# A residual quantizer on one core: constants on other engines, an overlap copied instead of loaded, and a third add by DMA

## The chip, the cores and the metric

The kernel runs on one core of a Trainium2 chip. The metric is the device time of one execution in microseconds.

## The reference

The input `x` has 2 sequences of 16000 positions with 512 channels, in bf16. The reference computes

- `z = silu(x[t-1]*w0 + x[t]*w1 + x[t+1]*w2)`, a depthwise convolution with three taps for each channel;
- four stages of residual quantization: for each position the nearest of 8 code words of the stage (by `|r|^2 - 2 r.c + |c|^2`, the first one on a tie) is taken from the residual `r`, which starts as `z`; the sum of the four chosen words is `q`;
- `y`, the same kind of three-tap convolution over `q` with the decoder's taps.

All roundings to bf16 on the way count, since a choice of word depends on them.

## The kernel before

The 32000 positions are laid out as 128 rows of 250 groups: row `p` holds positions `250 p` to `250 p + 249`, and group `g` is the 128 positions `250 p + g`. The 250 groups are worked in 17 chunks (`SIZES`: 4, 12, fourteen of 16, and 10). Channels lie on the partitions in four blocks of 128 (`i` = 0 to 3).

For each chunk:

- **Loading.** The buffer `XT` (two of them) holds the chunk's groups and one neighbour on each side, transposed. Chunks 0 and 1 come as rows (`RES` is borrowed for them), are transposed by TensorE (L366) and copied by VectorE and ScalarE (L371, L373). From chunk 2 on, SP's queue issues one DMA transpose per group, G + 2 for a chunk of G (L395).
- **Front.** Per block: three products `Z`, `T`, `T` (VectorE, L449), two additions into `Z` (either a DMA that adds, issued by POOL, or VectorE: L455, L457), the exponential, `+1` and reciprocal on ScalarE (L461, L466, L162; the `+1` of block 3 on VectorE, L468), and the product with `Z` into `RES` (VectorE, L476). From chunk 2 on, the first addition of every block goes by DMA, and the second one in blocks 0 and 1 (`DMA_ADDS`, `DMA_MORE`).
- **Four stages.** TensorE multiplies the residual with itself and with the code words (L540, L545); VectorE takes the norms (L553) and ScalarE the products (L556) out of PSUM; six small steps of VectorE find the first nearest word (L574 to L601); the one-hot is turned (L611, L618) and made into pairs (L626, L631); TensorE picks the words, in three bf16 parts `W` for each pair of words (L653); VectorE updates the residual (L659).
- **Output.** TensorE multiplies the one-hots with the decoder's words (L676), ScalarE copies them out of PSUM into `YSB` (two buffers, L682), and SP's queue stores them (L686).

Constants are made at the start: the mask and the presets of `KEY` and `OH`, the code columns in `RES` (`code_columns`, L227 and L228), the spreads, the word pairs (`pair_rows`, `pair_words`, L278 to L293) and the decoder's words (`taps_of`, `on_words`).

The order of the instructions on each engine is written down by a planner (`Plan.run`) while the kernel is built. Each task has an engine, a time that it holds it, a delay to its result, needs, a due time and buffers that it takes and gives. The planner plays the tasks forward in time and lets each engine take, of those that are ready, the one with the earliest due time. Planner engines such as `ACC`, `OUT`, `ROWS` and `WORDS` are only names: a DMA add is issued by POOL but planned on `ACC`, a store is issued by SP but planned on `OUT`. The order is then fixed: at run time each engine works through its list and waits where something isn't there. Due times come from `PERIOD` (of a chunk), `LEAD`, `SPREAD` (between blocks), `AFTER` (reciprocals), `STAGE` (between stages) and `LATE` (output).

Of the kernel before, what the change touches and what calls it, by code (L numbers as in the profile page):

```python
# [11 lines left out]
F32 = mybir.dt.float32  # L12
ALU = mybir.AluOpType
ACT = mybir.ActivationFunctionType
# [4 lines left out]
GC = 16  # L19
# [4 lines left out]

SIZES = [4, 12] + [16] * 14 + [10]

# [96 lines left out]
def kernel(  # L123
# [46 lines left out]
    for n, G in enumerate(SIZES):  # L170
# [7 lines left out]
    CB4 = const.tile([P, D], BF16, name="CB4")  # L178
    nc.sync.dma_start(out=CB4, in_=bass.AP(tensor=codebooks.tensor, offset=codebooks.offset,
                                             ap=[[0, J], [D, NC], [1, D]]))  # L180
# [44 lines left out]

    def code_columns(t):
        nc.vector.tensor_copy(t[:, :, :, 0:LC], CBT[:, :, :, 0:LC].to_broadcast([P, KT, 2 * GC, LC]))  # L227
        nc.vector.tensor_copy(t[:, :, :, LC + HT:], CBT[:, :, :, LC:].to_broadcast([P, KT, 2 * GC, LC]))  # L228

# [23 lines left out]
    def mask():  # L253
        for h in range(2):
            for r in range(GB):
                nc.vector.tensor_scalar(out=MASK[h * HT:(h + 1) * HT, r, :], in0=IDENT[h * HT:(h + 1) * HT, h * HT:(h + 1) * HT],
                                        scalar1=-1.0, scalar2=-FAR, op0=ALU.add, op1=ALU.mult)
# [22 lines left out]

    def pair_words(s):
        t = ypool.tile([P, J, D], out.dtype, name="YSB").rearrange("p j d -> p (j d)")
        full, left = t[:, 0:2 * D].bitcast(F32), t[:, 2 * D:4 * D].bitcast(F32)
        ends = t[:, 0:2 * D].rearrange("p (d e) -> p d e", e=2)
# [3 lines left out]
        nc.vector.tensor_scalar(out=ends[:, :, 0], in0=low, scalar1=-1.0, scalar2=None, op0=ALU.mult)  # L288
        nc.vector.tensor_tensor(out=ends[:, :, 1], in0=third, in1=high, op=ALU.subtract)
        nc.vector.tensor_copy(low, full)  # L290
        nc.vector.tensor_tensor(out=left, in0=full, in1=low, op=ALU.subtract)
        nc.vector.tensor_copy(high, left)
        nc.vector.tensor_tensor(out=third, in0=left, in1=high, op=ALU.subtract)  # L293

# [6 lines left out]
    def presets(n):  # L301
        for c in range(C):
            nc.vector.memset(KEYS[n][1][:, :, c, 0], float(C - c))
        nc.vector.memset(OHB[n], 0.0)

# [10 lines left out]
    def taps_of(name):  # L316
        t, first, tap, count = PARTS[name]
        nc.vector.memset(t, 0.0)
        src = bass.AP(tensor=dw_dec.tensor, offset=dw_dec.offset + tap * D, ap=[[D, count], [0, NC], [1, D]])
        nc.gpsimd.dma_start(out=t[first * NC:(first + count) * NC, :], in_=src)  # L320
# [5 lines left out]
    early = -4.0 * PERIOD  # L326
    words_in = plan.add("WORDS", 3.5, 3.5, [], early, lambda: None)
    codes = [plan.add("DVE", 0.3, 0.5, [words_in], early, code_words)]
    codes[0] = plan.add("DVE", 1.2, 1.4, codes, early + 2.0, lambda: code_columns(RESB[0]))
    scored = [plan.add("DVE", 2.4, 2.6, [], early + 1.0, mask), plan.add("DVE", 1.9, 2.1, [words_in], early + 1.0, code_norms)]  # L330
    preset = [plan.add("DVE", 0.8, 1.0, [], early + 2.0 if n == 0 else 0.1 * PERIOD, lambda n=n: presets(n)) for n in range(3)]
    spread = plan.add("DVE", 1.5, 1.7, [], 0.2 * PERIOD, spreads)
    words = []
    for n in range(Nq - 1):
        t = plan.add("DVE", 0.2, 6.0, [], (0.05 + 0.3 * n) * PERIOD, lambda n=n: pair_rows(n))
        words.append(plan.add("DVE", 5.0, 5.2, [t], (0.3 + 0.35 * n) * PERIOD, lambda n=n: pair_words(n), take=("Y",), give=("Y",)))
    codes.append(plan.add("DVE", 1.2, 1.4, [codes[0]], 0.1 * PERIOD, lambda: code_columns(RESB[1])))
    decoder = []
    for n, name in enumerate(PARTS):
        t = plan.add("DVE", 0.2, 6.0, [], (0.3 + 0.02 * n) * PERIOD, lambda name=name: taps_of(name))  # L340
        decoder.append(plan.add("DVE", 0.35, 0.45, [t], 0.5 * PERIOD, lambda name=name: on_words(name)))
    DEC = {name: v[0] for name, v in PARTS.items()}
# [12 lines left out]
    def load_rows(st, org):  # L355
# [29 lines left out]
    def load(st, org):  # L385
        g0, G, GP = st["g0"], st["G"], st["GP"]
        done = []
        if st["n"] < 2:
            load_rows(st, org)
            return  # L390

        def one(n):
            if n == 0:
                st["XT"] = xpool.tile([P, KT, GC + 2, P], BF16, name="XT")
            nc.sync.dma_start_transpose(out=st["XT"][:, :, n, :], in_=group_rows(g0 + n - 1))  # L395

        def edge(n):
            st["XE"] = const.tile([P, KT, P], BF16, name="XE")
            nc.sync.dma_start_transpose(out=st["XE"], in_=group_rows(0))

        def shift(n):
            XT, XE = st["XT"], st["XE"]
            nc.gpsimd.tensor_copy(XT[:, :, n, 0:P - 1], XE[:, :, 1:P])
            for b in range(B):
                p = (b + 1) * HB - 1
                nc.gpsimd.memset(XT[:, :, n, p:p + 1], 0.0)
            if GP > G:
                nc.gpsimd.memset(XT[:, :, G + 2:GP + 2, :], 0.0)

        for n in range(G + 2):  # L410
            due = org - 2.2 * PERIOD + 0.01 * n
            inside = 0 <= g0 + n - 1 < S
            t = plan.add("SP", 1.4, 2.2, done[-1:], due, (lambda n=n: one(n)) if inside else (lambda n=n: edge(n)),
                         take=("XT",) if n == 0 else ())
            done.append(t)
            if not inside:
                st["edge"] = plan.add("POOL", 1.0, 1.4, [t], due, lambda n=n: shift(n))
        st["loaded"] = [done[-1], st.get("edge")]

    def front(st, org):  # L420
# [20 lines left out]
        def block(i):  # L441
# [78 lines left out]
    def stage(st, s, due):  # L520
# [39 lines left out]
        for n in range(banks):  # L560
            m = -(-(G - q) // (banks - n))
            needs = [st["new"][i] for i in range(KT)]
            needs += scored[0:2] + ([codes[st["n"]]] if st["n"] < 3 else [])
            t = plan.add("PE", 0.05 + 0.25 * m, 0.25 + 0.25 * m, needs, due, lambda q=q, m=m: score(q, m), take=("psG",),
                         give=("RES",) if s == Nq - 1 and q + m == G else (), use=0.7)
# [211 lines left out]
```

## Time and profile before

| | |
|---|---|
| median of 3 runs | 797.56 us (787.12 to 799.63) |
| profiled execution | 797.84 us, span 796.1 us, mean granted clock 0.900 |
| busy: VectorE, ScalarE, TensorE | 672.9, 575.3, 565.2 us |
| DMA adds by POOL, transposes, stores of 512 KB | 90, 264, 61 |

In the lines, PE is TensorE, PEld its weight loads, DVE VectorE, ACT ScalarE, POOL GpSimd and SP the engine whose queue issues most of the DMAs. A group's row has its line, engine, operation, tiles and count, then busy time and the mean ns of one, then the idle time just before and what ended it. A row of waits has the total, the count and the longest.

### The profile page before, as it was taken

The page shows a single profiled execution, that of the slowest core. Times are in us where ns is not written, and L with a number is a line of the kernel's source. Part 1 is how long each engine was busy: PE and PEld are TensorE (multiplying, and loading weights), DVE is VectorE, ACT ScalarE, POOL GpSimd, SP SyncE. Part 2 cuts the span into 40 slices and gives each one's busy share as a digit, 9 for nine tenths or more (in the row PEclk, how much of TensorE's full clock was granted, in tenths as well). Part 3 has the DMA queues.
Part 4 walks back from the last instruction along what each step waited for, and adds up shares of the span by engine and source line. Part 5 has one row for each costly group of instructions (what it writes and reads, how often), then busy time and mean ns, then how long its engine had stood idle before and what let it go on. Part 6 is the DMA issues. An engine that isn't in the chain of part 4 may idle for free. (4 is left out here: it accounts for less than half of the span.)

```text
span 796.1 us, 24168 instructions
## 1 busy us (share of the span) xinstructions
PE 565.2 (71%) x10688; PEld 323.2 (41%) x10751; DVE 672.9 (85%) x1249; ACT 575.3 (72%) x658; POOL 98.4 (12%) x116
## 2 busy tenths in 40 slices
PE   3036776667667677777786877777774887888885
PEld 3012443244433444343444444444532444454542
DVE  4899688988978998698978999999995999999851
ACT  1519763869489795779779597989684898777454
POOL 1301002010201101010110111011110121100000
PEclk9557799769899999899988999989997899999999
DMA  7614869795999998899996799899989864422133
GB/s 194 113 26 76 164 100 177 143 155 127 169 159 203 201 168 144 175 172 187 138 229 137 132 203 174 172 203 190 193 144 195 145 166 115 114 75 81 55 135 133
DMA packets 167571, 119.08 MB, mean 150 GB/s; under 512 B 146921, under 2 KB 147306, under 8 KB 167338
## 3 DMA queue, kind: packets, MB, share of 16 engines
q1 hardware_dynamic: 153252, 69.77, 42.9%
q0 software_dynamic: 14064, 47.63, 34.6%
q8 instruction: 84, 1.38, 0.7%
q14 instruction: 21, 0.17, 0.1%
q10 hardware_dynamic: 150, 0.13, 0.1%
HBM read 3.70 MB, written 32.77 MB: 46 GB/s over the span
## 5 line engine op out<-in xcount | busy, mean ns | idle before, releaser
L659 DVE TENSOR_TENSOR RES<-RES,SEL 128x2048 bf16<-128x2048 bf16 (+2 forms) x204 | 222.5, 1137 | 29.9 <-PE SEL L653 29.4
L545 PEld LDWEIGHTS <-RES 128*64 128x64 bf16 x8064 | 164.2, 117 | 113.6 <-issue 84.0
L545 PE MATMUL PS<-RES 128*64 128x80 bf16 (+1 forms) x8064 | 189.8, 207 | 21.1 <-DVE RES L476 11.3
L653 PE MATMUL SEL<-OHP,W 64*128 64x512 bf16 (+2 forms) x1224 | 159.3, 393 | 33.6 <-ACT OHP L631 12.6
L455 POOL DMA_DIRECT2D Z<-T x90 | 86.3, 973 | 579.2 <-ACT PR L556 83.4
L682 ACT ACTIVATE YSB<-Y 128x1024 bf16<-128x1024 f32 (+1 forms) x126 | 125.7, 1025 | 31.2 <-DMA out_dram<-YSB 14.6
L461 ACT ACTIVATE E<-Z 128x2048 bf16<-128x2048 bf16 (+2 forms) x68 | 121.5, 1789 | 27.1 <-DVE Z L457 26.0
L553 DVE TENSOR_REDUCE TR<-PS 128x6 bf16<-128x384 f32 (+2 forms) x188 | 95.3, 510 | 30.3 <-PE PS L545 16.9
L162 ACT ACTIVATE E<-E 128x2048 bf16<-128x2048 bf16 (+2 forms) x68 | 119.4, 1787 | 0.2
L556 ACT ACTIVATE PR<-PS 128x48 bf16<-128x48 f32 (+2 forms) x188 | 37.2, 209 | 106.5 <-PE PS L545 68.5
L653 PEld LDWEIGHTS <-W 64*128 64x128 bf16 x1224 | 61.6, 100 | 108.8 <-issue 71.0
L449 DVE TENSOR_SCALAR T<-XT,WENC 128x2048 bf16<-128x2048 bf16 (+2 forms) x136 | 96.5, 717 | 9.5 <-DMA Z<-T 8.7
L676 PE MATMUL Y<-A,OHT 128*128 128x512 bf16 x225 | 79.7, 393 | 20.0 <-ACT YSB L682 7.4
L540 PE MATMUL PS<-MASK,IDENT 128*128 128x384 bf16 (+2 forms) x188 | 61.6, 328 | 44.6 <-ACT PR L556 23.5
L466 ACT ACTIVATE E<-E 128x2048 bf16<-128x2048 bf16 (+2 forms) x51 | 90.9, 1787 | 0.2
L476 DVE TENSOR_TENSOR RES<-Z,E 128x2048 bf16<-128x2048 bf16 (+2 forms) x68 | 77.4, 1140 | 3.4 <-ACT E L162 3.2
L676 PEld LDWEIGHTS <-OHT 128*128 128x128 bf16 x373 | 33.1, 99 | 66.7 <-issue 31.3
L457 DVE TENSOR_TENSOR Z<-Z,T 128x2048 bf16<-128x2048 bf16 (+2 forms) x46 | 46.8, 1018 | 7.7 <-DMA Z<-T 7.7
L611 PE MATMUL ps_oh<-IDENT,OH 128*128 128x128 bf16 x252 | 27.2, 231 | 36.7 <-DVE OH L601 31.0
L449 DVE TENSOR_SCALAR Z<-XT,WENC 128x2048 bf16<-128x2048 bf16 (+2 forms) x68 | 48.4, 714 | 5.6 <-issue 5.3
L350 PE MATMUL PS<-CB,IDENT 128*128 128x512 bf16 x130 | 45.5, 444 | 7.8 <-ACT PR L556 6.3
L618 ACT ACTIVATE OHT<-ps_oh 128x512 bf16<-128x512 bf16 (+2 forms) x68 | 38.2, 566 | 16.1 <-PE ps_oh L611 15.6
(87 smaller groups left out, 389.7 us busy)
## 6 DMA issues: line engine op xcount, KB each, us to landing
Z<-T POOLq DMA_DIRECT2D x84, 512.0 KB, 6.5
out_dram<-YSB SPq DMA_DIRECT2D x61, 512.0 KB, 4.1
XT<-in_x_dram SPq DMA_TRANSPOSE x263, 4.4
Z<-T POOLq DMA_DIRECT2D x6, 384.0 KB, 5.1
RES<-in_x_dram SPq DMA_DIRECT2D x1, 1536.0 KB, 11.2
RES<-in_x_dram SPq DMA_DIRECT2D x1, 640.0 KB, 6.4
W<-in_codebooks_dram POOLq DMA_DIRECT2D x6, 64.0 KB, 5.5
W<-in_codebooks_dram POOLq DMA_DIRECT2D x3, 128.0 KB, 5.2
```

The source lines that it names most:

```text
L162: nc.scalar.add_instruction(mybir.InstActivation(name=nc.get_next_instruction_name(), engine=mybir.EngineType.Activation, ins=args, outs=[ ...
L449: nc.vector.tensor_scalar(out=places(u[name]), in0=taps(i, k), scalar1=WENC[:, i, k:k + 1], scalar2=None, op0=ALU.mult)
L455: nc.gpsimd.dma_start(out=z, in_=t, accum_op=ALU.add)
L461: nc.scalar.activation(u["E"][:, 0:G, :], u["Z"][:, 0:G, :], ACT.Exp, scale=-1.0)
L466: nc.scalar.activation(e, e, ACT.Copy, bias=1.0)
L476: nc.vector.tensor_tensor(out=st["RES"][:, i, 0:2 * G, LC:LC + HT], in0=halves(u["Z"]), in1=halves(u["E"]), op=ALU.mult)
L545: nc.tensor.matmul(V[h * HT:(h + 1) * HT, r, :], lhsT=half[:, LC:LC + HT], rhs=half[:, lo:hi], start=False, stop=(i == KT - 1), skip_group ...
L553: nc.vector.tensor_reduce(out=u["TR"][:, q:q + m], in_=u["V", q][:, :, own:own + HT], axis=AX.X, op=ALU.max)
L653: nc.tensor.matmul(SEL[:, r, 0:R * HT], lhsT=WORDS[s][k][rows, i * P:(i + 1) * P], rhs=u["OHP"][rows, 0:R * HT], start=(k == 0), stop=(k = ...
L659: nc.vector.tensor_tensor(out=now, in0=now, in1=sel[:, :, 0:G, :], op=ALU.add)
L676: nc.tensor.matmul(Y[:, h, :], lhsT=lhs(), rhs=rhs, start=(a == 0), stop=(a == len(terms) - 1))
L682: nc.scalar.activation(u["YSB"][:, k:k + n, :], u[k][:, 0:n, :], ACT.Copy)
```

## The change

- **Constants.** The mask, the presets and the zeroing of the decoder's words go from VectorE to POOL. Of the eight steps for each word pair, three go from VectorE to ScalarE (`even_end` and the two `part`; `guard`, `odd_end` and `remainder` stay on VectorE), and the steps are planned one by one, the first pair at the start. The spreads and the code columns are due at the start.
- **Start.** The codebook is loaded from ScalarE's queue, the two small row pieces from SP's queue, ahead of the large ones.
- **Third chunk's transposes.** Chunk 2 takes its `XT` only after chunk 1's rows have theirs.
- **Two groups copied.** From chunk 2 on, the first two groups of `XT` are copied by ScalarE from the last two of the chunk before (L431, `overlap`), so that a chunk of G groups needs G transposes: 234 instead of 264.
- **One more add by DMA.** `DMA_MORE` is 3: the second addition of block 2 goes by DMA too, 105 instead of 90.
- **Order.** DMA adds are planned on POOL, stores on SP beside the transposes; times and due times are others. TensorE's list has the same work, with 157 filler products instead of 150 (L350); ScalarE has one more pair of table loads.

```diff
-DMA_MORE = 2
+DMA_MORE = 3
-SWITCH, AFTER = 1.3, 0.6
-PERIOD, LEAD, STAGE, LATE, SPREAD = 56, 0, 0.9, 0.3, 0.2
+SWITCH, AFTER = 1.3, 0.86
+PERIOD, LEAD, STAGE, LATE, SPREAD = 56.0, 0.51, 0.67, 0.75, 0.24
...
-    nc.sync.dma_start(out=CB4, in_=...)
+    nc.scalar.dma_start(out=CB4, in_=...)
...
-    nc.sync.dma_start(out=XR[:, 1:G + 2, :], in_=xv[:, 0:G + 1, :])
     for b in range(B):
         p = b * HB
-        nc.scalar.dma_start(out=XR[p + 1:p + HB, 0, :], in_=xv[p:p + HB - 1, S - 1, :])
+        nc.sync.dma_start(out=XR[p + 1:p + HB, 0, :], in_=xv[p:p + HB - 1, S - 1, :])
+    nc.sync.dma_start(out=XR[:, 1:G + 2, :], in_=xv[:, 0:G + 1, :])
...
-                nc.vector.tensor_scalar(out=MASK[...], ...)
+                nc.gpsimd.tensor_scalar(out=MASK[...], ...)
...
-    def pair_words(s):
-        ...
+    def guard(s):
+        ...
+    def even_end(s):
+        t = halves_of[s] = ypool.tile([P, J, D], out.dtype, name="YSB").rearrange("p j d -> p (j d)")
+        nc.scalar.activation(t[:, 0:2 * D].rearrange("p (d e) -> p d e", e=2)[:, :, 0], WORDS[s][0], ACT.Copy, scale=-1.0)
+    def odd_end(s):
+        ...
+    def part(s, k):
+        full, left = halves_of[s][:, 0:2 * D].bitcast(F32), halves_of[s][:, 2 * D:4 * D].bitcast(F32)
+        nc.scalar.activation(WORDS[s][k], left if k else full, ACT.Copy)
+    def remainder(s, k):
+        ...
...
-            nc.vector.memset(KEYS[n][1][:, :, c, 0], float(C - c))
-        nc.vector.memset(OHB[n], 0.0)
+            nc.gpsimd.memset(KEYS[n][1][:, :, c, 0], float(C - c))
+        nc.gpsimd.memset(OHB[n], 0.0)
...
-        nc.vector.memset(t, 0.0)
+        nc.gpsimd.memset(t, 0.0)
...
-        rows = plan.add("ROWS", 0.1 + 0.9 * G, 0.1 + 0.9 * G, [], early + org, room, take=("XT",))
+        rows = plan.add("ROWS", 6.5, 6.5, [], early + org, room, take=("XT",))
+        st["rows"] = rows
...
+        last = chunks[st["n"] - 1]
+
+        def overlap():
+            k = last["G"]
+            nc.scalar.activation(st["XT"][:, :, 0:2, :], last["XT"][:, :, k:k + 2, :], ACT.Copy)
+
-        for n in range(G + 2):
+        for n in range(2, G + 2):
             due = org - 2.2 * PERIOD + 0.01 * n
             inside = 0 <= g0 + n - 1 < S
-            t = plan.add("SP", 1.4, 2.2, done[-1:], due, (lambda n=n: one(n)) if inside else (lambda n=n: edge(n)),
-                         take=("XT",) if n == 0 else ())
+            t = plan.add("SP", 1.7, 1.7, done[-1:] + ([last.get("both"), last.get("rows")] if n == 2 else []), due,
+                         (lambda n=n: one(n)) if inside else (lambda n=n: edge(n)), take=("XT",) if n == 2 else ())
...
+        done.append(plan.add("BANK", 0.0, 3.0, done[-1:], due, lambda: None))
+        st["both"] = plan.add("ACT", 1.0, 1.1, [done[0]] + last["loaded"], org - 0.4 * PERIOD, overlap)
-        st["loaded"] = [done[-1], st.get("edge")]
+        st["loaded"] = [done[-1], st.get("edge"), st["both"]]
...
-                    return plan.add("ACC", 1.2 + 1.8 * f, 7.5, needs, due, lambda: total(k), give=("T",))
+                    return plan.add("POOL", 1.2 + 1.8 * f, 7.5, needs, due, lambda: total(k), give=("T",))
...
-            t = plan.add("PE", 0.05 + 0.25 * m, 0.25 + 0.25 * m, needs, due, lambda q=q, m=m: score(q, m), ...)
+            t = plan.add("PE", 0.05 + 0.215 * m, 0.25 + 0.215 * m, needs, due, lambda q=q, m=m: score(q, m), ...)
...
-            maxima.append(plan.add("ACT", 0.25, 0.38, [t], due, lambda q=q, m=m: dots(q, m)))
+            maxima.append(plan.add("ACT", 0.11, 0.25, [t], due, lambda q=q, m=m: dots(q, m)))
...
-            st["new"][i] = plan.add("DVE", 0.07 + 1.15 * f, 0.17 + 1.15 * f, [c] + seen, due, lambda i=i: subtract(i), give=("psA",))
+            st["new"][i] = plan.add("DVE", 0.065 + 1.066 * f, 0.18 + 1.066 * f, [c] + seen, due, lambda i=i: subtract(i), give=("psA",))
...
-        plan.add("OUT", 1.5, 3.0, [c], due, store, give=("Y",))
+        plan.add("SP", 0.5, 4.0, [c], due, store, give=("Y",))
```

More of the change, by code (lines that the diff above doesn't have):

```diff
@@ L279, in pair_rows @@
         nc.gpsimd.dma_start(out=WORDS[s][1], in_=odd)
-    def pair_words(s):
-        t = ypool.tile([P, J, D], out.dtype, name="YSB").rearrange("p j d -> p (j d)")
-        full, left = t[:, 0:2 * D].bitcast(F32), t[:, 2 * D:4 * D].bitcast(F32)
-        ends = t[:, 0:2 * D].rearrange("p (d e) -> p d e", e=2)
+    halves_of = {}
+    def guard(s):
         low, high, third = WORDS[s]
@@ L326 @@
     early = -4.0 * PERIOD
-    words_in = plan.add("WORDS", 3.5, 3.5, [], early, lambda: None)
+    words_in = plan.add("WORDS", 4.0, 4.0, [], early, lambda: None)
     codes = [plan.add("DVE", 0.3, 0.5, [words_in], early, code_words)]
     codes[0] = plan.add("DVE", 1.2, 1.4, codes, early + 2.0, lambda: code_columns(RESB[0]))
-    scored = [plan.add("DVE", 2.4, 2.6, [], early + 1.0, mask), plan.add("DVE", 1.9, 2.1, [words_in], early + 1.0, code_norms)]
-    preset = [plan.add("DVE", 0.8, 1.0, [], early + 2.0 if n == 0 else 0.1 * PERIOD, lambda n=n: presets(n)) for n in range(3)]
@@ L332 @@
-    spread = plan.add("DVE", 1.5, 1.7, [], 0.2 * PERIOD, spreads)
+    scored = [plan.add("POOL", 3.6, 3.8, [], early + 2.5, mask), plan.add("DVE", 1.9, 2.1, [words_in], early + 1.0, code_norms)]
+    preset = [plan.add("POOL", 1.2, 1.4, [], early + (3.0, 5.0, 6.0)[n], lambda n=n: presets(n)) for n in range(3)]
+    spread = plan.add("DVE", 1.5, 1.7, [], early + 3.0, spreads)
     words = []
     for n in range(Nq - 1):
-        t = plan.add("DVE", 0.2, 6.0, [], (0.05 + 0.3 * n) * PERIOD, lambda n=n: pair_rows(n))
-        words.append(plan.add("DVE", 5.0, 5.2, [t], (0.3 + 0.35 * n) * PERIOD, lambda n=n: pair_words(n), take=("Y",), give=("Y",)))
@@ L337 @@
-    codes.append(plan.add("DVE", 1.2, 1.4, [codes[0]], 0.1 * PERIOD, lambda: code_columns(RESB[1])))
+        due = early + 1.5 if n == 0 else 0.2 * n * PERIOD
+        t = plan.add("POOL", 1.7, 7.0, [], due, lambda n=n: pair_rows(n))
+        t = plan.add("DVE", 0.9, 1.1, [t], due + 7.0, lambda n=n: guard(n))
+        t = plan.add("ACT", 0.5, 0.7, [t], due + 8.0, lambda n=n: even_end(n), take=("Y",))
+        t = plan.add("DVE", 0.65, 0.75, [t], due + 9.0, lambda n=n: odd_end(n))
+        for k in range(2):
+            t = plan.add("ACT", 0.5, 0.7, [t], due + 10.0 + 2.0 * k, lambda n=n, k=k: part(n, k))
+            t = plan.add("DVE", 0.62, 0.75, [t], due + 11.0 + 2.0 * k, lambda n=n, k=k: remainder(n, k), give=("Y",) if k else ())
@@ L338 @@
+        words.append(t)
+    codes.append(plan.add("DVE", 1.2, 1.4, [codes[0]], early + 4.0, lambda: code_columns(RESB[1])))
     decoder = []
     for n, name in enumerate(PARTS):
-        t = plan.add("DVE", 0.2, 6.0, [], (0.3 + 0.02 * n) * PERIOD, lambda name=name: taps_of(name))
-        decoder.append(plan.add("DVE", 0.35, 0.45, [t], 0.5 * PERIOD, lambda name=name: on_words(name)))
+        t = plan.add("POOL", 0.9, 6.0, [], (0.4 + 0.02 * n) * PERIOD, lambda name=name: taps_of(name))
+        decoder.append(plan.add("DVE", 0.35, 0.45, [t], 0.8 * PERIOD, lambda name=name: on_words(name)))
```

27 lines of the change are left out of this document (13 added, 14 removed).

## The prediction, made before the result was known

> **What bounds the kernel now.** I read the page first, then busy time by stretches, then VectorE's groups and waits, then the start and the DMA queues.
>
> ```profile
> span 796.1 us, 24168 instructions
> PE 565.2 (71%) x10688; PEld 323.2 (41%) x10751; DVE 672.9 (85%) x1249; ACT 575.3 (72%) x658; POOL 98.4 (12%) x116
> q1 hardware_dynamic: 153252, 69.77, 42.9%
> q0 software_dynamic: 14064, 47.63, 34.6%
> ```
>
> VectorE (DVE) is the fullest engine. The two DMA queues together are busy 77.5% of sixteen engines' span, so the transfers are no small matter either. Busy time by stretch (span of the stretch, then PE, PEld, DVE, ACT, POOL, granted clock, DMA share, GB/s):
>
> ```profile
> 0.00:53.00 53.00, 11.68 (x124) 10.02 (x126) 38.39 (x132) 14.08 (x18) 11.11 (x23) 0.71 0.54 115
> 200.00:550.00 350.00, 260.08 (x5127) 147.26 (x5154) 311.85 (x530) 279.92 (x314) 46.20 (x50) 0.93 0.99 175
> 700.00:796.10 96.10, 78.07 (x1497) 44.01 (x1506) 64.38 (x132) 59.69 (x88) 0.86 (x1) 0.99 0.26 99
> L476 DVE TENSOR_TENSOR RES<-Z,E 128x2048 bf16<-128x2048 bf16 x32 | 39.0, 1218 | 0.9 <-ACT E L162 0.9
> ```
>
> The last row is VectorE's group of final silu multiplies in 200 to 550 us. There are four for each chunk, so 32 are eight chunks in 350 us: 43.75 us a chunk, of which VectorE works 39.0 (89%), ScalarE 35.0 (80%), and the DMA share is 0.99. The steady part is thus set by VectorE's queue and its waits, with the DMA engines close behind. What VectorE waited for in 100 to 700 us:
>
> ```profile
> DVE RES L659 <- PE SEL L653: 18.2, 21, 4.4
> DVE TR L553 <- ACT PR L556: 12.8, 11, 8.9
> DVE T L449 <- DMA Z<-T: 8.7, 5, 4.3
> DVE Z L457 <- DMA Z<-T: 7.7, 2, 4.8
> ...
> DVE T L449 <- DMA XT<-in_x_dram: 0.8, 1, 0.8
> ```
>
> The one wait of 8.9 us is a transfer in disguise. In the timeline:
>
> ```profile
> 596.17 7.69 SPq L395 DMA_TRANSPOSE XT<-in_x_dram  x2
> ...
> 610.70 1.94 ACT L682 ACTIVATE YSB<-Y 128x1024 bf16<-128x1024 f32 x2 [9.99 <-DMA out_dram<-YSB]
> 612.77 0.56 DVE L553 TENSOR_REDUCE TR<-PS 128x6 bf16<-128x384 f32 x1 [8.87 <-ACT PR L556]
> ```
>
> Two slow transposes (3.8 us each) hold SP's queue, the store behind them is late, ScalarE stands 9.99 us for the output buffer, and VectorE stands 8.87 us behind ScalarE. So the DMA-linked waits of VectorE are 8.7 + 7.7 + 0.8 + 8.9 = 26.1 us.
>
> **The change part by part.** All terms go against the profiled execution's own 797.84 us (span 796.1 and 1.7 around it); the median of the three timed runs, 797.56, is the same within 0.3 us.
>
> Constants. Groups over the whole span (busy us, mean ns):
>
> ```profile
> L288 DVE TENSOR_SCALAR YSB<-W 128x512 bf16<-128x512 bf16 x3 | 1.3, 448 | 0.0
> L290 DVE CAST W<-YSB 128x512 bf16<-128x512 f32 x3 | 1.3, 428 | 0.1
> L292 DVE CAST W<-YSB 128x512 bf16<-128x512 f32 x3 | 1.3, 427 | 0.1
> L318 DVE MEMSET A<- 128x256 uint32 x4 | 1.1, 272 | 0.0
> L303 DVE MEMSET KEY<- 128x16 bf16 x24 | 1.6, 72 | 0.1
> L304 DVE MEMSET OH<- 128x256 uint32 x3 | 0.8, 272 | 0.0
> L270 DVE CAST SPREADS<-OWN 128x64 bf16<-128x64 f32 x3 | 0.6, 191 | 0.0
> L271 DVE CAST SPREADS<-OWN 128x64 bf16<-128x64 f32 x3 | 0.6, 187 | 0.0
> L227 DVE COPY RES<-CBT 128x2048 bf16<-128x2048 bf16 x3 | 2.0, 682 | 0.0
> ```
>
> And two rows of the timeline:
>
> ```profile
> 12.62 0.23 DVE L223 TENSOR_SCALAR CBT<-ps_cbt 128x128 bf16<-128x128 bf16 x1 [7.05 <-PE ps_cbt L222]
> ...
> 69.46 0.95 DVE L457 TENSOR_TENSOR Z<-Z,T 128x1536 bf16<-128x1536 bf16 x1
> ```
>
> VectorE stands 7.05 us until 12.62 us, when the first rows have arrived; chunk 1's last add begins at 69.46. The mask and two of the three presets ran before that, in time that was free, so moving them is worth nothing. Worth something is what ran after it. Three of the eight steps of each `pair_words` go to ScalarE: 3 x 1.3 = 3.9. The tap memsets go to POOL: seven of 0.272, 1.9. So does the third preset, 2.4 / 3 = 0.8. The spreads go forward into the wait: 1.2. One pair of code columns also fits into it, now that TensorE turns the codebook before the x rows: 1.4. Together 9. Bounds: 0, if VectorE merely waits for what now comes from elsewhere, and 9.
>
> Against it: pair 0 of the words now crosses between VectorE and ScalarE six times, and the constants are work on POOL while VectorE runs. What the latter costs, one place shows:
>
> ```profile
> 2.17 0.32 POOL masks.py:199 TENSOR_SCALAR_AFFINE_SELECT IDENT<-IDENT 128x128 bf16<-128x128 bf16 x1
> ...
> 646.73 0.61 POOL L403 COPY XT<-XE 128x508 bf16<-128x508 bf16 x1 [0.28 <-DMA XE<-in_x_dram]
> 646.74 1.14 DVE L449 TENSOR_SCALAR Z<-XT,WENC 128x2048 bf16<-128x2048 bf16 x1
> 647.47 1.34 POOL L408 MEMSET XT<- 128x1024 bf16 x1
> 647.94 1.41 DVE L449 TENSOR_SCALAR T<-XT,WENC 128x2048 bf16<-128x2048 bf16 x1
> 650.12 0.74 DVE L449 TENSOR_SCALAR Z<-XT,WENC 128x2048 bf16<-128x2048 bf16 x1
> ```
>
> The same product takes 0.74 us alone and 1.14 and 1.41 beside POOL's copy and memset: 1.07 lost beside about 2.0 of POOL work, a half. POOL's new constants I estimate from the memset (1.34 us for 1024 elements a row) and from the short operation at 2.17 us (0.32): 12 of the mask 3.6, 24 small memsets at no more than that, say 6, three of 512 elements 2, seven of 512 for the taps 4.7, together 16. Much of that falls ahead of 12.6 us or beside reads of PSUM. I take 4 for both costs; bounds 0 and 8 (half of 16).
>
> The third chunk's transposes. Before, SP takes the second XT buffer for chunk 2 at once:
>
> ```profile
> 2.48 73.44 SPq L395 DMA_TRANSPOSE XT<-in_x_dram  x23
> ```
>
> So chunk 1 has to wait until chunk 0 lets its buffer go. Afterwards chunk 1 gets it and chunk 2 waits. That moves chunk 1's front forward and puts chunk 2's sixteen transposes behind chunk 0's last product. VectorE is not idle in between either way (38.39 busy of 53.00 with the first 12 us empty), so I book nothing; if chunk 2 is late, the gain of the constants is what is lost, which their bound of 0 holds.
>
> The third add by DMA. It takes one L457 add from each of chunks 2 to 16, fourteen full and one of 1536:
>
> ```profile
> L457 DVE TENSOR_TENSOR Z<-Z,T 128x2048 bf16<-128x2048 bf16 x28 | 34.1, 1218 | 7.7 <-DMA Z<-T 7.7
> L682 ACT ACTIVATE YSB<-Y 128x1024 bf16<-128x1024 f32 x124 | 124.6, 1032 | 29.8 <-DMA out_dram<-YSB 13.2 <-PE Y L676 11.7 <-PE SEL L653 1.8
> ```
>
> With 0.95 for the smaller one (the row at 69.46), 14 x 1.218 + 0.95 = 18.0 us of VectorE. At its 89% share of the steady part 16 of them are time; bounds 0 (the waits grow by what the work shrinks) and 18.
>
> Two groups copied per chunk. This adds 15 copies of 128x1024 on ScalarE, near the 1.03 us of the row above: 15 us on an engine with 20% to spare. Behind a copy stand exponentials and score copies; the copy waits for the buffer and for the last transposes of the chunk before. I take 2; bounds 0 and 15.
>
> DMA load and order. An add costs 34.6% x 796.1 / 90 = 3.06 us of all sixteen engines; 705 to 796 us, with stores alone on q1, gives the rest:
>
> ```profile
> q1 hardware_dynamic: 2470, 8.41, 23.3%
> out_dram<-YSB SPq DMA_DIRECT2D x15, 512.0 KB, 3.3
> ```
>
> That is 21.2 us for some 16 stores, 1.33 each. Of q1's 341 us over the span stores are 83, and the 264 transposes at most 258, about 0.95 each. So the change adds 15 x 3.06 = 46 and removes 30 x 0.95 = 28: 17 more, 1.2 a chunk on 43.3. Against that, the new plan knows better what a transfer takes: it holds SP for a transpose 1.7 and puts the stores on that same queue, where before both ran as if on separate ones. I take a quarter of the 26.1 us of DMA-linked waits as gone, -6; bounds -26 (all gone) and +26 (doubled).
>
> Tail: one more stage of a full chunk is ordered behind the last silu, but the work is the same, and VectorE has 32 of 96 us free there. I book nothing; bounds 0 and 5 (its four updates at the 1.22 of an add of that shape).
>
> Sum: 797.84 - 9 + 4 - 16 + 2 - 6 = 772.8, so 773.
>
> **The rivals.**
>
> Nearly all transfers' waits go. Then -9 + 2 - 18 + 1 - 22 gives 752. For it: the waits hang on few places; against it: the load rises.
>
> The add's time turns into waits. Then L659's waits for TensorE and the wait for the adds grow by 16, and only the start's 5 and some 3 of the order are left: 790. For it: 18.2 us of waits for SEL that no add touches.
>
> The DMA engines become the bound; this is the slow side. It decides if the share can't rise above the 0.99 of the steady part. Then a chunk takes (43.3 + 1.2) / 0.99 = 45.0 us, 1.2 longer than 43.75, 17 over 14 chunks. The rows at 603 us say what a full queue does; another such stall costs 8.9. With the start's 5 gained: 797.8 - 5 + 17 + 9 = 819. For it: the share, and adds that land late. Against it: single stretches already have more than 0.99.
>
> ```profile
> 250.00:300.00 50.00, 35.91 (x757) 21.56 (x761) 45.58 (x77) 44.61 (x50) 7.44 (x8) 0.96 1.05 184
> L455 POOL DMA_DIRECT2D Z<-T x90 | 86.3, 973 | 579.2 <-ACT PR L556 83.4 <-DVE T L449 60.6 <-DMA Z<-T 41.9
> ```
>
> POOL blocks VectorE in full. If each microsecond of POOL's 16 of constants and of 15 more issues at 0.97 (15) stopped VectorE, 31 would be lost in place of 4: 800. The half that the rows at 647 us show speaks against it.
> The Trainium skill (SBUF — State Buffer, Who interferes with whom) has this as its rule: the port pair that VectorE and GpSimd share is an exclusive lock, and the later one stops fully. The trace agrees on the kind (0.74 against 1.41) but not on a full stop.
>
> **How the numbers follow.** Forecast 773, its own range 757 to 788: 0.46. Transfers' waits gone (752): 0.17. Add turned into waits (790): 0.18. POOL blocks (800): 0.05. DMA bound (819): 0.14. Two per cent, which is about what a measurement of this kernel tells from no change, is below 781.6 for faster and above 813.5 for slower. Faster: 0.17 and nearly all of the first, 0.44, 0.61. Slower: 0.14. Within: 0.25. The range goes from 750, under the first rival, to 802, over POOL's, and leaves out the DMA case.
>
> **What would show it.** VectorE's busy time near 673 - 18 - 9 = 646 or up to 4 above; L457 in 31 instead of 46; chunk period near 42.5; the DMA share over 0.99 without more waits of VectorE on Z<-T or of ScalarE on the store; chunk 1's adds done by about 60 us, not 70. Wrong if the waits of VectorE on SEL, PR or Z<-T grow by 15 or more, if ScalarE stands at the copies, or if VectorE's products are stretched through the first 30 us.

## The result, and the profile after

The changed kernel takes 746.41 us (median of four runs, 745.04 to 753.73) where the kernel before takes 795.41 (787.12 to 799.63): a ratio of 0.9435, 95% interval 0.9327 to 0.9544. Forecast were 773, with a range of 750 to 802: the side is right, the gain (49 us for 25) twice as large as forecast, and the time lies below the range. Medians here are over all runs of a kernel; ratios and their intervals leave out runs that took over 1.5% longer than the fastest run of the same kernel.

The page of the changed kernel, and its busy time by stretches (columns as in the prediction). The profiled execution took 753.73 us, the longest of the four.

```profile
span 751.9 us, 24290 instructions
PE 562.7 (75%) x10758; PEld 319.7 (43%) x10758; DVE 644.5 (86%) x1179; ACT 594.9 (79%) x684; POOL 122.2 (16%) x177
...
q1 hardware_dynamic: 136944, 65.83, 43.3%
q0 software_dynamic: 16224, 55.36, 41.4%
```

```profile
0.00:53.00 53.00, 9.91 (x96) 8.59 (x96) 41.10 (x93) 26.59 (x32) 20.73 (x68) 0.72 0.40 110
53.00:76.00 23.00, 17.76 (x248) 10.08 (x250) 20.01 (x47) 15.14 (x19) 5.84 (x5) 0.72 0.79 146
76.00:100.00 24.00, 12.29 (x191) 6.39 (x190) 12.01 (x25) 13.82 (x14) 2.57 (x3) 0.78 1.24 151
200.00:550.00 350.00, 281.96 (x5531) 158.22 (x5532) 317.29 (x559) 302.67 (x342) 55.18 (x58) 0.94 1.03 188
```

Of the 44.2 us that the span loses, VectorE's work accounts for 28.4 (672.9 to 644.5) and its idle time for 15.8 (123.2 to 107.4). The steady part is fuller on every engine at once: TensorE 282 in place of 260 us of 350, ScalarE 303 for 280, VectorE 317 for 312, and the DMA share is 1.03.

VectorE's last final multiply of chunks 1 and 2, before and then after, with chunk 1's last additions and the transposes behind chunk 0's front:

```profile
79.69 0.94 DVE L476 TENSOR_TENSOR RES<-Z,E 128x1536 bf16<-128x1536 bf16 x1
...
111.61 1.23 DVE L476 TENSOR_TENSOR RES<-Z,E 128x2048 bf16<-128x2048 bf16 x1 [0.40 <-ACT E L162]
```

```profile
29.59 85.72 SPq L412 DMA_TRANSPOSE XT<-in_x_dram  x47
...
53.49 1.94 DVE L483 TENSOR_TENSOR Z<-Z,T 128x1536 bf16<-128x1536 bf16 x2
...
69.11 0.95 DVE L502 TENSOR_TENSOR RES<-Z,E 128x1536 bf16<-128x1536 bf16 x1
...
115.44 1.22 DVE L502 TENSOR_TENSOR RES<-Z,E 128x2048 bf16<-128x2048 bf16 x1
```

Chunk 1 is done 10.6 us earlier, and chunk 2 is 3.8 us later: its transposes start only at 29.59 us and run on, with those of the next chunks, to 115 us, 1.8 us each, and in 76 to 100 us VectorE works 12.0 of 24 us. At that point nothing is gained; the gain comes after it. How late chunk 2 is belongs to this one execution: in three variants below that start alike (`k_add2`, `k_tr1`, `k_ld1`) its last multiply ends at 111 to 112 us, where the kernel before has 112.8 and this execution 116.7.

The waits of the changed kernel over the whole span (total, times, longest):

```profile
DVE RES L685 <- PE SEL L679: 23.5, 20, 4.8
ACT XT L431 <- DMA XT<-in_x_dram: 13.4, 2, 9.7
ACT YSB L708 <- DMA out_dram<-YSB: 12.3, 6, 5.1
PE SEL L679 <- ACT YSB L708: 7.6, 9, 2.5
DVE Z L483 <- DMA Z<-T: 5.7, 3, 2.3
```

### The profile page after: what moved, and what is told of

Its sections match the earlier page's. It is cut to its first block, busy times and chain, and to the rows that moved or that the text cites. A ratio compares the mean times of both kernels' runs of the same rounds, so it can differ in the third digit from the quotient of the medians.

```text
span 751.9 us, 24290 instructions
## 1 busy us (share of the span) xinstructions
PE 562.7 (75%) x10758; PEld 319.7 (43%) x10758; DVE 644.5 (86%) x1179; ACT 594.9 (79%) x684; POOL 122.2 (16%) x177
## 4 chain that ended last, share of the span: by engine, by line
DVE 31%; ACT 27%; PE 13%; DMA 12%; SPq 11%; issue 4%; ACTq 0%; POOL 0%; DVEq 0%; POOLq 0%
DVE RES L685 12%; SPq L412 11%; ACT E L162 6%; ACT E L487 6%; ACT YSB L708 6%; DMA Z<-T 5%; PE PS L571 5%; DVE TR L579 4%; ACT E L492 3%; DVE T L475 3%; PE Y L702 3%; DMA out_dram<-YSB 3%; PE SEL L679 3%; DVE RES L502 3%; DMA XT<-in_x_dram 2%
## 5 line engine op out<-in xcount | busy, mean ns | idle before, releaser
L685 DVE TENSOR_TENSOR RES<-RES,SEL 128x2048 bf16<-128x2048 bf16 (+2 forms) x204 | 221.5, 1136 | 24.2 <-PE SEL L679 23.5
L481 POOL DMA_DIRECT2D Z<-T x105 | 99.4, 966 | 514.5 <-DVE T L475 98.0
L679 PE MATMUL SEL<-OHP,W 64*128 64x512 bf16 (+2 forms) x1224 | 153.5, 381 | 30.8 <-ACT OHP L657 12.8
L702 PE MATMUL Y<-A,OHT 128*128 128x512 bf16 x249 | 84.0, 382 | 10.9 <-ACT YSB L708 5.5
L502 DVE TENSOR_TENSOR RES<-Z,E 128x2048 bf16<-128x2048 bf16 (+2 forms) x68 | 77.5, 1140 | 5.8 <-ACT E L162 5.8
L366 PE MATMUL PS<-CB,IDENT 128*128 128x512 bf16 x157 | 50.8, 431 | 10.1 <-ACT PR L582 10.1
L702 PE MATMUL Y<-B,OHT 128*128 128x512 bf16 x124 | 47.3, 381 | 2.7 <-ACT OHT L644 2.7
L652 PE MATMUL ps_pair<-OHT,SPREADS 32*64 32x256 bf16 (+2 forms) x408 | 21.2, 284 | 23.1 <-ACT OHT L644 21.6
```

The source lines that it names most:

```text
L481: nc.gpsimd.dma_start(out=z, in_=t, accum_op=ALU.add)
L502: nc.vector.tensor_tensor(out=st["RES"][:, i, 0:2 * G, LC:LC + HT], in0=halves(u["Z"]), in1=halves(u["E"]), op=ALU.mult)
L679: nc.tensor.matmul(SEL[:, r, 0:R * HT], lhsT=WORDS[s][k][rows, i * P:(i + 1) * P], rhs=u["OHP"][rows, 0:R * HT], start=(k == 0), stop=(k = ...
L685: nc.vector.tensor_tensor(out=now, in0=now, in1=sel[:, :, 0:G, :], op=ALU.add)
L702: nc.tensor.matmul(Y[:, h, :], lhsT=lhs(), rhs=rhs, start=(a == 0), stop=(a == len(terms) - 1))
```

## The experiments

The first question was which part carries the gain: the third addition by DMA, the 30 transposes, the order, or the constants. The kernels named "replanned" let the planner lay out a new order; the others keep the changed kernel's order and alter one thing in it.

**The third addition, replanned.**

```diff
-DMA_MORE = 3
+DMA_MORE = 2
```

> The changed kernel with two second additions by DMA per chunk instead of three. Theory (VectorE's work sets the time, so its 18.0 us for 15 additions are time): 746 + 16 to 18, 762 to 764. Rival (the order made the gain, and the third addition only turns into waits for the DMA): 744 to 750.

768.25 us (750.90 to 784.69, four runs). The runs spread over 34 us, from near the changed kernel's time up, so they settle nothing, and the same question was asked again in the order kept.

**The third addition, in the order kept.** First on VectorE, at the place in the order where GpSimd issued it; then left out.

```diff
-                if k <= adds:
+                if k <= adds and not (i == 2 and k == 2):
```

> The changed kernel, every engine's order kept, but the second addition of block 2 done by VectorE in the place of the list where POOL's DMA was planned. Theory (18.0 us of VectorE's work are time, nearly one for one): 760 to 764. Rival (that work only fills waits): 746 to 752. If the DMA it takes away was a load that hurt: below 746.

746.13 us, ratio 0.9391, interval 0.9323 to 0.9458: the same as the changed kernel. The page of this variant and its steady part:

```profile
span 744.8 us, 24275 instructions
PE 561.9 (75%) x10758; PEld 318.1 (43%) x10758; DVE 660.3 (89%) x1194; ACT 594.4 (80%) x684; POOL 108.3 (15%) x162
```

```profile
200.00:550.00 350.00, 283.24 (x5614) 159.10 (x5615) 331.92 (x574) 307.83 (x348) 47.90 (x51) 0.96 0.92 179
```

VectorE has 15.8 us more to do (660.3), and the span isn't longer: its idle time is 84.5 where the changed kernel has 107.4 (an estimate for a run of its median time is 100). The DMA share falls from 1.03 to 0.92.

```diff
+                if i == 2 and k == 2 and not early:
+                    return
```

> The changed kernel, order kept, with block 2's second addition left out altogether from chunk 2 on (the third tap of that block is missing in the result): 15 DMA additions less, and nothing in their place. Theory (VectorE's 18 us and the DMA's 46 us of sixteen engines cancelled when the addition was moved back): 725 to 735. Rival (neither matters, both fill waits): 742 to 748.

738.94 us, ratio 0.9286, interval 0.9260 to 0.9311. Without the 15 additions the kernel is 7.5 us faster than with them on DMA and 7.2 faster than with them on VectorE. By the ratios the two differences are 12 and 8, with errors (95%) of some 9 and 6. So 15.8 us of VectorE's work are worth 7 or 8 us, about half, and fifteen additions by DMA cost 7 to 12, much the same within the errors. Between the two ways the ratios leave 4 us in VectorE's favour with an error of 10: the 16 that were booked as gain are outside it.

**The order.** The changed kernel with the due times of before, then with the planner's old engines and durations, then one due time shifted by a hundredth of a period:

```diff
-SWITCH, AFTER = 1.3, 0.86
-PERIOD, LEAD, STAGE, LATE, SPREAD = 56.0, 0.51, 0.67, 0.75, 0.24
+SWITCH, AFTER = 1.3, 0.6
+PERIOD, LEAD, STAGE, LATE, SPREAD = 56, 0, 0.9, 0.3, 0.2
```

> The changed kernel with the due times of before (AFTER 0.6, LEAD 0, STAGE 0.9, LATE 0.3, SPREAD 0.2). Theory (the waits that went, some 16 to 20 us, went by the due times): 762 to 766. Rival A (they went because the planner now prices transfers and queues as they are): 746 to 750. Rival B (the order is the whole gain): above 775.

789.67 us (773.56 to 793.65); its lowest run is 20 us above the changed kernel's highest.

```diff
-                    return plan.add("POOL", 1.2 + 1.8 * f, 7.5, ...)
+                    return plan.add("ACC", 1.2 + 1.8 * f, 7.5, ...)
...
-        plan.add("SP", 0.5, 4.0, [c], due, store, give=("Y",))
+        plan.add("OUT", 1.5, 3.0, [c], due, store, give=("Y",))
...
(transposes 1.4 and 2.2; scores, dots and updates at their old durations)
```

> The changed kernel with its due times, but with the planner's old engines and times in the steady part (additions on ACC, stores on OUT 1.5/3.0, transposes 1.4/2.2, score 0.25, dots 0.25, update 1.15). Theory (due times): 746 to 750. Rival A (the planner's prices): 760 to 766.

767.59 us, ratio 0.9627, interval 0.9562 to 0.9692: some 15 us lost.

```diff
-PERIOD, LEAD, ... = 56.0, 0.51, ...
+PERIOD, LEAD, ... = 56.0, 0.50, ...
```

> The changed kernel with LEAD 0.50 in place of 0.51, nothing else: the same work, and a hundredth of a period in the fronts' due times. Theory (due times as such, the rules of the new plan): 742 to 750. Rival D (the order on record is one good draw among many; a neighbour of it is an ordinary one): 760 to 785.

751.46 us, ratio 0.9465, interval 0.9397 to 0.9533: a neighbouring order does as well, which speaks against a lucky draw, though one neighbour is little.

Then the other way: the kernel before, with nothing but the new due times and the planner's new engines and durations.

> The kernel before with the changed kernel's due times and the planner's engines and times of the steady part; constants, transposes, copies and additions as before. Theory (the order is worth some 20 us by itself): 772 to 778. Rival (it is worth nothing without the rest): 790 to 800. Rival D (a new order is a new draw): anywhere from 760 to 810.

774.44 us, ratio 0.9648, interval 0.9577 to 0.9719: the order alone takes off 22 to 34 us. Its page and two of its waits:

```profile
PE 577.9 (75%) x10796; PEld 322.7 (42%) x10796; DVE 666.0 (87%) x1249; ACT 574.5 (75%) x658; POOL 97.9 (13%) x116
```

```profile
DVE Z L449 <- DMA XT<-in_x_dram: 20.6, 5, 4.8
DVE RES L659 <- PE SEL L653: 18.2, 20, 4.8
```

VectorE's wait for TensorE's selections is 18.2 in place of 29.4 over the whole span before. What is left are 20.6 us in which the first product of a chunk waits for its transposes: the queue that the copies relieve. Between the last multiplies of chunks 4 and 13 a chunk takes 42.0 us here, no more than the 42.1 of the changed kernel's profile, though there are still eighteen transposes for each.

**The 30 transposes.** Eighteen per chunk again, replanned, then in the order kept (three transposes in place of each chunk's first, no copy).

> The changed kernel without the copied groups: G + 2 transposes per chunk again, 15 copies of ScalarE less. Theory (the copies are free, and the 30 transposes of some 0.95 us of all DMA engines are worth little): 744 to 752. Rival C (the shorter transfer queue took the waits away): 758 to 770.

800.34 us, ratio 1.0046, interval 0.9994 to 1.0097: no gain over before at all.

```diff
-            nc.sync.dma_start_transpose(out=st["XT"][:, :, n, :], in_=group_rows(g0 + n - 1))
+            for m in ((0, 1, 2) if n == 2 else (n,)):
+                nc.sync.dma_start_transpose(out=st["XT"][:, :, m, :], in_=group_rows(g0 + m - 1))
...
-            nc.scalar.activation(st["XT"][:, :, 0:2, :], last["XT"][:, :, k:k + 2, :], ACT.Copy)
+            return
```

> The changed kernel, every engine's order kept, but ScalarE's 15 copies left out and the two groups loaded again: three DMA transposes in the place of the first one of each chunk. Theory (the 800 of the version that was planned anew came from its order, not from the 30 transposes): 742 to 756. Rival C (the 30 transposes hold SP's queue and the DMA engines, and that is where the time goes): 785 to 800.

781.66 us, ratio 0.9816, interval 0.9764 to 0.9868: 35 us lost by the medians, 30 by the ratios. Its waits, and one place of its timeline:

```profile
DVE RES L686 <- PE SEL L680: 45.4, 23, 9.6
ACT YSB L709 <- DMA out_dram<-YSB: 38.1, 12, 10.0
PE SEL L680 <- ACT YSB L709: 32.8, 10, 9.8
```

```profile
202.52 26.26 SPq L413 DMA_TRANSPOSE XT<-in_x_dram  x14
...
217.50 1.92 ACT L709 ACTIVATE YSB<-Y 128x1024 bf16<-128x1024 f32 x2
...
228.88 0.64 SPq L713 DMA_DIRECT2D out_dram<-YSB  x1
...
235.41 1.02 ACT L709 ACTIVATE YSB<-Y 128x1024 bf16<-128x1024 f32 x1 [9.96 <-DMA out_dram<-YSB]
...
236.49 2.74 PE L680 MATMUL SEL<-OHP,W 64*128 64x512 bf16 x12 [9.83 <-ACT YSB L709]
...
237.99 2.50 DVE L686 TENSOR_TENSOR RES<-RES,SEL 128x2048 bf16<-128x2048 bf16 x2 [9.56 <-PE SEL L680]
```

Read it from the top. Fourteen transposes hold SP's queue for 26.26 us, 1.88 each. The first of the two copies at 217.50 us fills the output buffer, by 218.5; its store goes out at 228.88, ten us after it could have gone, and lands some 6 us later. ScalarE needs that output buffer and stands 9.96 us; TensorE's next selections write into PSUM that ScalarE has not yet emptied, and stand 9.83; VectorE's updates stand 9.56. One chain, four engines, and its root is a queue that no engine's busy time shows. Beside it VectorE's first products wait 11 us for their transposes in this variant, and not at all in the changed kernel.

**Is it the queue, or the DMA engines?** The median times from issue to landing, changed kernel first, then this variant:

```profile
out_dram<-YSB SPq DMA_DIRECT2D x61, 512.0 KB, 4.6
XT<-in_x_dram SPq DMA_TRANSPOSE x233, 5.3
```

```profile
out_dram<-YSB SPq DMA_DIRECT2D x61, 512.0 KB, 3.7
XT<-in_x_dram SPq DMA_TRANSPOSE x263, 4.7
```

With 30 transposes more, a transfer lands no later once it is issued; the time is lost ahead of the issue. Taken store by store from the traces, the first 40 stores stand ready for 131 us in all before SP issues them in the changed kernel, and for 221 us in this variant. To ask it by runs as well, first the stores were moved to ScalarE's queue, with eighteen and with sixteen transposes.

```diff
-            nc.sync.dma_start(out=outv[:, g:g + len(groups), :], in_=u["YSB"][:, 0:len(groups), :])
+            nc.scalar.dma_start(out=outv[:, g:g + len(groups), :], in_=u["YSB"][:, 0:len(groups), :])
```

> The version with 18 loads per chunk in the changed kernel's order (782), but the stores issued from ScalarE's queue instead of SP's. Theory (30 more transposes cost 35 us because the stores stand behind them in SP's queue: store late, output buffer late, ScalarE, TensorE's SEL, VectorE): 745 to 757, with ScalarE's wait for the store near that of the changed kernel. Rival (it is the DMA engines' load, whoever issues): 772 to 785.

> The changed kernel, order kept, stores issued from ScalarE's queue. Theory (some 12 us of ScalarE's wait for the store are left in it, and each store costs ScalarE's queue about half a us): 738 to 746. Rival (issuing 64 stores holds ScalarE by more than it saves): 750 to 765.

810.73 us (ratio 1.0169, interval 1.0118 to 1.0221) and 799.57 (1.0032, 0.9994 to 1.0071): far from either theory. A new wait took the place of the old one, as the timeline of the second shows on ScalarE:

```profile
289.32 1.90 ACT L492 ACTIVATE E<-E 128x2048 bf16<-128x2048 bf16 x1
298.36 0.34 ACTq L712 DMA_DIRECT2D out_dram<-YSB  x1
298.75 0.20 ACT L582 ACTIVATE PR<-PS 128x40 bf16<-128x40 f32 x1 [7.53 <-DMA XT<-in_x_dram]
```

The store's own issue waits for an earlier transpose to land, since both use one semaphore: in the trace the wait is for the semaphore numbered 118, it ends at 298.32 us, and a transpose with the same semaphore has landed at 298.28. Now it is ScalarE that stands behind it, six times by 5 to 10 us, 44 in all in the profiled execution; by its median the variant loses 53. These two runs say nothing on the question, so it was put in another way: one transfer of 128 KB more per chunk, ahead of the chunk's first transpose, into a tile that nobody reads, once transposing and once plain; and seventeen transposes per chunk.

```diff
+            if n == 2:
+                nc.sync.dma_start_transpose(out=SCRAP, in_=group_rows(g0))
```

> The changed kernel in its own order, with one transpose by DMA more per chunk (15 in all), put just ahead of each chunk's first in the queue and landing in a tile that nobody reads; ScalarE's copy of the two groups stays. If the 30 transposes that the change removes cost their 35 us by holding SyncE's queue, some 1.2 us for each, 15 of them cost about half of it: 761 to 767 us, with ScalarE's waits for the store and VectorE's for SEL growing by some 10 each. If what cost was that ScalarE and VectorE wait for three landings instead of one at the chunk's first products, this kernel has none of that: 744 to 752.

```diff
+            if n == 2:
+                nc.sync.dma_start(out=SCRAP.rearrange("p k t -> p (k t)"), in_=group_rows(g0))
```

> The same with a plain load in the transpose's place: the same 128 KB from the same rows, from the same queue, into the same unread tile, but no transposing. If the queue's hold by the transposing form costs, this one is cheap: 744 to 753. If the sixteen DMA engines' load costs (15 x 0.9 us of them), it costs as much as the transposes: 758 to 767, both kernels alike.

```diff
+            for m in ((1, 2) if n == 2 else (n,)):
+                nc.sync.dma_start_transpose(out=st["XT"][:, :, m, :], in_=group_rows(g0 + m - 1))
...
-            nc.scalar.activation(st["XT"][:, :, 0:2, :], last["XT"][:, :, k:k + 2, :], ACT.Copy)
+            nc.scalar.activation(st["XT"][:, :, 0:1, :], last["XT"][:, :, k:k + 1, :], ACT.Copy)
```

> The changed kernel in its own order, with one of the two shared groups transposed again and one copied: 17 transposes per chunk where the changed kernel has 16 and the variant without copies has 18 (781.7). A steady price per transpose gives half of that variant's 35 us: 760 to 768. If the price is in a threshold (the queue's work per chunk passes its room only with the 18th), 746 to 755; if leaving out the copy is what cost (the first products wait for DMA alone), also 746 to 755, since a copy is still there.

| variant | transposes per chunk | median, us | ratio, interval |
|---|---|---|---|
| changed kernel | 16 | 746.4 | 0.9435, 0.9327 to 0.9544 |
| one plain load more | 16 | 747.4 | 0.9403, 0.9332 to 0.9473 |
| one unread transpose more | 17 | 757.6 | 0.9508, 0.9423 to 0.9594 |
| one copied, one transposed | 17 | 768.9 | 0.9649, 0.9560 to 0.9738 |
| none copied | 18 | 781.7 | 0.9816, 0.9764 to 0.9868 |

The queue of SP in the variant with the unread transpose, then in the one with the plain load, each with the median time from issue to landing:

```profile
316.56 1.96 SPq L415 DMA_TRANSPOSE SCRAP<-in_x_dram  x1
...
SCRAP<-in_x_dram SPq DMA_TRANSPOSE x15, 9.3
```

```profile
308.93 0.42 SPq L415 DMA_DIRECT2D SCRAP<-in_x_dram  x1
...
SCRAP<-in_x_dram SPq DMA_DIRECT2D x15, 128.0 KB, 9.1
```

The same bytes land after the same time; in these rows the transposing form holds the queue 1.96 us, the plain one 0.42 (medians of the fifteen: 2.19 and 0.58). The plain one costs nothing that can be told within an error of 10 us. Seventeen transposes lie a little over half way between sixteen and eighteen, so the price looks steady, with no threshold in sight.

The pair with the unread transfer is weaker than it looks. The unread transpose's 757.6 us lies between the two times that were expected. By the ratios it differs by 8 us with an error of 9, and the waits that were to grow by some 10 with the unread transpose did not, beside 23.5 and 12.3 in the changed kernel:

```profile
DVE RES L689 <- PE SEL L683: 24.2, 24, 4.8
ACT YSB L712 <- DMA out_dram<-YSB: 14.6, 8, 5.1
```

The SP timeline shows a reason. Nothing reads the tile, so its transpose goes out while SP would otherwise stand waiting for the chunk's buffer; in 9 of 15 chunks SP still stands for over 1 us after it, and the hold cost the queue nothing, as here:

```profile
444.86 1.84 SPq L415 DMA_TRANSPOSE SCRAP<-in_x_dram  x1
457.70 4.50 SPq L416 DMA_TRANSPOSE XT<-in_x_dram  x3
```

The first 40 stores stand ready for 137 us in this variant, 5 more than in the changed kernel, and for 177 where the seventeenth transpose takes the copy's place, 46 more. So the unread transpose tests the queue in a part of the chunks only, and its 11 us (6 by the ratios, with an error of 11) are not shown to be the price of the hold. The evidence for the queue is the variants with 17 and 18, both clear of noise, their stores, and the landings; how the 22 and 35 us divide between late stores and first products that wait for their transposes stays open.

**The constants.** The codebook first in SP's queue again, so that VectorE can start earlier; then the mask, the presets and the zeroing back on VectorE.

```diff
-    nc.scalar.dma_start(out=CB4, in_=...)
+    nc.sync.dma_start(out=CB4, in_=...)
```

> The changed kernel, order kept, with the codebook loaded from SP's queue first, ahead of the rows, as before. VectorE waits 9.4 us for it at the start of the changed kernel. Theory (the start is VectorE's, so some 4 us of it come through): 740 to 744. Rival (chunk 2's transposes set the time by 90 us, so an earlier start is waited away): 745 to 748.

745.6 us, ratio 0.9357, interval 0.9313 to 0.9402: nothing that can be told from the changed kernel.

```diff
-                nc.gpsimd.tensor_scalar(out=MASK[...], ...)
+                nc.vector.tensor_scalar(out=MASK[...], ...)
...
(the memsets of KEY, OH and of the decoder's words likewise)
```

> The changed kernel in its own order, but the mask, the presets and the zeroing of the decoder's words on VectorE again, at the places in the order that they have now. VectorE has about 4.3 us more to do after its first rows are there (three presets of 0.8, seven memsets of 0.27; the mask falls into its first wait), and loses the 2.3 us by which its first products are stretched beside GpSimd. If constants are worth what the prediction booked (9 gained, 4 lost, of which these parts are some 3 gained and most of the 4 lost): 745 to 749. If the chunk that follows waits for its transposes anyway, as after the codebook's earlier load, nothing: 744 to 747. If the start's VectorE time goes through in full and GpSimd's constants cost nothing: 750 to 752.

753.68 us, ratio 0.9490, interval 0.9425 to 0.9555, against 0.9327 to 0.9544 for the changed kernel: about 4 us are lost if anything, within the error of both. Only these three constants went back; the steps moved to ScalarE and the earlier start of the others were not tried apart.

## Why the prediction was too small

*The mechanism* held in part: the DMA engines did not become the bound, and VectorE is still the fullest engine, but a microsecond of its work is only about half a microsecond of time, and its waits hang on SP's queue and on the order more than was booked. Their work rose by 20 us of sixteen engines (84.7% of 751.9 against 77.5% of 796.1; forecast 17), and the steady part simply ran at a share of 1.03. That the sum came out so near is luck: the additions' queue rose by 36 us where 46 was booked, the other queue fell by 16 where 28 was booked. The rival at 819 is out. Nearest came the rival at 752, by which the waits for transfers go: VectorE's waits on Z<-T, 16.4 us over the whole span before, are 7.0. Of the signs that were named, these came: VectorE's busy time 644.5 (forecast 646), the addition L483 on VectorE in 31 instead of 46, a share over 0.99, chunk 1's additions done at 55 us. The chunk period, forecast near 42.5, is 42.1 between the last multiplies of chunks 4 and 13 (44.3 before). ScalarE does not stand longer at the store either (12.3 us, 14.6 before).

*The add: -16 was wrong.* It multiplied VectorE's 18 us by its 89% share. The variants give 7 or 8 us for the work and about as much for the transfers that replace it, so nothing. That is near what the rival at 790 said (the work turns into waits). The step here is the price of a microsecond on an engine that is 89% busy: about half of it was on the path. This error made the forecast too fast; it hid part of the next two, and by luck 773 came as near as 27 us.

*The transposes: the term was missing.* The step that made the gain too small is the term "DMA load and order", -6, which stands for this and the next point. The prediction saw the very chain (store late behind two slow transposes, 9.99 us of ScalarE, 8.87 of VectorE), but counted the 30 removed transposes as 28 us of DMA engine time inside "DMA load and order", -6. Their price was the queue's time, some 1.8 us each (1.82 in the row at 29.59; single ones in the changed kernel from 1.19 to 5.09), and what stands behind it: 30 to 35 us when they are put back into this order. The Trainium skill (Advanced Engine Details and Errata, X-Bar Transpose (TRN2)) says that transposing transfers are as fast as regular ones: the landing agrees (9.3 and 9.1 us), and the hold of the queue (2.19 and 0.58) is a thing apart. The Trainium skill also says (DMA: Bandwidth & Descriptors, Issuing engines are not separate DMA queues) that the time it takes to start a DMA is usually small beside the DMA itself; here a transpose holds its queue for some 1.8 us, beside 5.3 to its landing and at most 0.95 of all sixteen engines by the prediction's estimate.

*The order: -6 was too small.* Alone it is worth 22 to 34. The quarter of the 26.1 us of DMA-linked waits that the prediction took had no row behind it. The order also shortens waits on engines, such as VectorE's for SEL, 18.2 for 29.4, which that term did not include.

*The parts don't add up*, and should not: 28 for the order alone and 30 to 35 for the transposes in the final order make some 60, and the whole is 49. Taken one after the other, the order comes first (795 to 774, or 767 by the ratio), and the copies with the constants bring the rest to 746. The price of the transposes is thus one in a given order: with the order alone, eighteen of them did not lengthen the chunk period (42.0), and by the two profiles nearly all that the changed kernel is faster by lies behind chunk 13: from its last multiply to chunk 16's pass 121.8 us with the order alone and 105.0 in the changed kernel. Why it lies there is open. Why the replanned order with eighteen transposes (800) is worse than the kernel before with the new order (774) stays open: its due times are those that suit sixteen, and nothing here separates that from the draw of an order.

*The constants: -9 and +4* leave -5. Only a part was tested, by `k_const`: about 4 us with an error of 10, so neither these terms nor the codebook's earlier load can be told from nothing. The bound of 0 was there for the case that chunk 2 is late, and in the profiled execution it is late by 3.8 us. GpSimd's memsets stretched what VectorE did beside them, as rows of the changed kernel's timeline show (in the kernel before, the same line has a mean of 0.69):

```profile
15.15 0.98 POOL L327 MEMSET A<- 128x512 bf16 x1
...
15.59 1.09 DVE L228 COPY RES<-CBT 128x2048 bf16<-128x2048 bf16 x1
...
18.70 0.97 POOL L327 MEMSET A<- 128x512 bf16 x1
...
19.13 1.09 DVE L228 COPY RES<-CBT 128x2048 bf16<-128x2048 bf16 x1
```

Each copy runs beside the memset for some 0.54 us and takes 0.40 longer, three quarters of the time together. In the prediction's rows at 647 us it was 1.07 us of the 1.88 in which both ran. So the stretch is short of a full stop, and more than half.

*The copies: +2.* They are 1.07 us each in the steady part, as booked, and in the profiled execution ScalarE stands at two of the fifteen only, 13.4 us in all, 9.7 of them before 95 us, where the first chunks' transposes are late. From 200 to 550 us it stands at none:

```profile
L431 ACT ACTIVATE XT<-XT 128x1024 bf16<-128x1024 bf16 x8 | 8.5, 1066 | 0.0
```

*The tail: 0.* After VectorE's last final multiply, which ends at 674.2 us, 78 us follow; before it ended at 729.1 and 67 followed. One more stage stands behind it, as ordered. Whether those 11 us are lost, or the work is only later, wasn't tried apart.

## What to carry to other kernels

Price a DMA by three things: its bytes, its landing, and how long its issue holds the queue; the third is in no engine's busy time, and whatever stands behind it in the queue (here a store, and by way of its buffer three engines) pays for it. Work taken from the fullest engine is worth its full time only where that engine ends every chain: here about half of it, and the DMAs that took it over cost about as much. An order laid out by a planner is as good as its durations and due times: new ones alone, for the same work, brought some 28 us, and the price of a queue's time is a price in one order.

## What the hardware showed

A transpose by DMA of 128 KB, put ahead of each chunk's first, holds the issuing queue 2.19 us (median; 1.26 to 2.97) and a plain load of the same rows 0.58, while both land after some 9 us. A store issued from ScalarE's queue waited for an earlier transpose from SP's queue to land (7.53 us in the row shown, 44 in all), through a semaphore that the program gave to both; another queue did not free it from the transposes, and that kernel is 53 us slower.
